# One expert-layer unit reordered: casts queued behind a PSUM copy, a subtraction moved up, weight casts started a step later

## The chip, the cores and the metric

The kernel runs on one core of a Trainium2 chip. The metric is the device time of one execution in microseconds (us); lower is better. Each time is a median of several runs.

## The reference, cut to what matters

The program adds three things: the input `x` of 2048 tokens by 512 features, a spectral filter of the normalised input, and a mixture of 8 experts on the normalised input. Only the experts matter for this change. All 8 experts are used for every token (the "top 8 of 8"), so the work is dense:

```
h = _gelu(jnp.einsum("nd,edf->nef", xt, w1))      # 512 -> 1792 per expert
y = jnp.einsum("nef,efd->ned", h, w2)             # 1792 -> 512
out = jnp.einsum("ne,ned->nd", cw, y)             # weighted by the gates cw
```

Everything is float32, and the result is compared at a precision that the kernel reaches by splitting each matmul operand in two parts.

## The kernel before, in words

**Split operands.** A float32 operand becomes a high part (a cast to the rounded type fp32r, on ScalarE) and a low part (operand minus high part, on VectorE or GpSimd). A product of two such operands is three passes of matmuls: low times high, high times low, high times high. In the code `high()` (L820 is its cast) and `low()` (L823 its subtraction) do this for an activation; `split()` (L549, L550) does it for a weight, with the subtraction on GpSimd.

**Chunks and units.** The 8 x 1792 hidden columns are cut in 56 chunks of 256. Eight chunks are done in the plain way in the first fifth of the run, beside the spectral branch. The other 48 chunks are taken two at a time, as 24 pairs `c`, and for each pair the tokens are taken in two parts `i`; so there are 48 **units** `u = 2c + i`. I call units with `i = 0` even and those with `i = 1` odd. Within a unit the first layer is a 2 x 2 block product done with seven products in place of eight (a Strassen-like scheme): the forms of the input (`b11`, `b21`, `b22`, `T1` to `T4`) lie ready in HBM and are loaded, the forms of the weights (`a11`, `a12`, `a22`, `s1` to `s4`) are made by GpSimd. The second layer is such a block product again, and runs one unit later.

**One product** (`product`, matmuls at L784) is twelve matmuls of 128 x 128 by 128 x 512 into one PSUM tile of 128 x 1024. A unit issues 14 products in this order, numbered P0 to P13 here: first-layer and second-layer products alternate, the second-layer ones being those of the unit before.

- P0 `a11*b11` into X (PSUM tile B); P1 second layer, `b22`; ScalarE copies X to Z (PSUM tile A, L803 `A<-B`).
- P2 `a12*b21` onto X, which the copy must have read by then; P3 second layer, `T3`, onto the tile of P1.
- P4 `s2*T2` onto Z, then a copy of Z to `s` (L803 `c<-A`); P5 second layer, `b11`.
- P6 `s1*T1` onto Z, which the copy to `s` must have read, then a copy to `h22`; P7 second layer, `b21`.
- P8 `s4*b22` onto Z; P9 second layer, `T1`; P10 `s3*T3` into a new tile; P11 second layer, `T4`; P12 `a22*T4`; P13 second layer, `T2`.

**The vector work of a unit.** `gelu` is L807, on ScalarE. `weigh` multiplies by the gates (L838, VectorE). `plus` (L813) adds PSUM to SBUF on VectorE; after every second-layer product it empties or reads the PSUM tile into `acc`, and the next product onto that tile must wait for it. `less` (L816) subtracts two SBUF tiles on VectorE. From the four activated blocks h11, s (the block 21), h22 and h12 these make the second layer's forms: h12 becomes form T3 (`less(h12, h22, h12)`), h11 becomes T1, h22 becomes T2, s becomes T4.

**What sets the order.** In the 48 units the instructions of TensorE, ScalarE and VectorE run in the order in which the code is written (`strict`, `pin`). `layer1` and `layer2` are generators, advanced by the loop at the end of the program: seven rounds of three steps of `layer1`, with one step of the second layer in between, and with some steps of weight preparation (`weights(n)`). In an even unit these prepare the second layer's weights of the pair (sums at L758 to L762, from the tile `raw` loaded as `in_wb`) and stand after the third step of a round; in an odd unit they prepare the first layer's weights of the next pair (L738 to L744, `in_wa`) and stand after the first step. GpSimd's subtractions are placed by the framework's scheduler, in the order of what they wait for. Loads go through one queue, SP's, in order.

Of the kernel before, what the change touches and what calls it, by code (L numbers as in the profile page):

```python
# [89 lines left out]
def r32(ap):  # L90
    return ap.bitcast(F32)
# [3 lines left out]
def body(ctx: ExitStack, tc: tile.TileContext, io):  # L95
    nc = tc.nc
# [6 lines left out]
    scratch = edge.tile([P, EDGE], F32, name="edge")  # L103
# [19 lines left out]
    def load(src):  # L123
        raw = keep.tile([P, 8 * FC], F32, name="raw")
        nc.sync.dma_start(raw, src)
        return raw
# [53 lines left out]
    last_pe, last_dve, last_act, last_pool, main_act, last_cast, last_sp = ([None] for _ in range(7))  # L180
# [149 lines left out]
    def gate(e, i):  # L330

        cb = rp.tile([P, 2, TB], F32, name="cwb", bufs=2)
        for j in range(2):
            c0 = (2 * j + i) * TB
            nc.sync.dma_start(cb[:, j, :], cwd[e, c0 : c0 + TB].partition_broadcast(P))
        return cb
# [208 lines left out]
    def pin(ins):  # L545
        return tc.keep_in_program_order(ins) if strict else ins
# [206 lines left out]
    def sums2(raw, tp, c):  # L753

        a11, a12, a21, a22 = (raw[:, i * F2 : (i + 1) * F2] for i in range(4))
        s1, s2, s4 = (tp.tile([P, F2], F32, name=n) for n in ("s1", "s2", "s4"))
        add = nc.gpsimd.tensor_tensor
        add(s1, a21, a22, op=ALU.add)  # L758
        add(s2, s1, a11, op=ALU.subtract)  # L759
        add(s4, a12, s2, op=ALU.subtract)  # L760
        yield [("s4", s4)] + [("a21", a21)] * (c + 1 == N2)
        add(a21, a21, a11, op=ALU.subtract)  # L762
        yield [("s3", a21)]
        yield [("a11", a11)]
        yield [("a12", a12)]
        yield [("s1", s1)]
        yield [("a22", a22)]
        yield [("s2", s2)]

    def prepare(pool, tag, items, to):  # L770

        for step in items:
            for n, src in step:
                to[n] = pool.tile([P, 2, 2, FC], F32R, name=f"{tag}{n}")
                split(to[n], src.rearrange("p (k f) -> p k f", k=2), nc.gpsimd)
            yield

    def product(pt, w, x, start):

        for m in range(2):  # L780
            n = 0
            for hw, hx in PASSES:
                for k in range(2):
                    pin(nc.tensor.matmul(  # L784
                        pt[:, m, :], w[:, hw, k, m * P : (m + 1) * P], x[:, hx, k, :], start=(start and n == 0), stop=(n == 5),
                        skip_group_check=not start,
                    ))
                    n += 1
# [3 lines left out]
    def bank(name):  # L792
        return pq.tile([P, 2, TB], F32, name=name)

    def xin(n, i):
        if (n, i) in ahead:
            return ahead.pop((n, i))
        x = xr.tile([P, 2, 2, TB], F32R, name="xr", bufs=3)
        nc.sync.dma_start(r32(x), xs[n][i])
        return x  # L800

    def copy_of(dst, src):
        last_act[0] = pin(nc.scalar.copy(dst, src)).ins  # L803
        return dst

    def gelu(v):
        last_act[0] = pin(nc.scalar.activation(v, v, AF.Gelu_apprx_tanh)).ins  # L807

    def tmp():
        return rp.tile([P, 2, TB], F32, name="c", bufs=5)  # L810

    def plus(dst, a, b):
        pin(nc.vector.tensor_add(dst, a, b))  # L813

    def less(dst, a, b):
        pin(nc.vector.tensor_sub(dst, a, b))  # L816

    def high(hs, n, src):
        hs[n] = rp.tile([P, 2, 2, TB], F32R, name="hs", bufs=4)
        main_act[0] = pin(nc.scalar.copy(hs[n][:, 0], src)).ins  # L820

    def low(hs, n, src, pool=False):
        op = (nc.gpsimd if pool else nc.vector).tensor_tensor(hs[n][:, 1], src, r32(hs[n][:, 0]), op=ALU.subtract)  # L823
        if not pool:
            pin(op)
        return op.ins

    def layer1(c, i, w, hs, old):

        last = (c, i) == (N2 - 1, 1)  # L830
        first = c == 0 and i == 0
        e = [ORDER[N1 + 2 * c + j] // NC for j in range(2)]
        cb = {}
        oh, o11, o21, o22, o12 = tuple(old) or (None,) * 5

        def weigh(dst, src, fh, nh):
            g = cb[e[fh]][:, nh : nh + 1, :].to_broadcast([P, 2, TB])
            pin(nc.vector.tensor_mul(dst, src, g))  # L838

        for j in sorted(set(e))[: 1 if first else 2]:  # L840
            cb[j] = gate(j, i)
        X = bank("B")
        x = xin("b11", i)
        product(X, w["a11"], x, True)
        Z = bank("A")
        if first:
            product(Z, w["a11"], x, True)
            ahead["T3", i] = xin("T3", i)
            nc.sync.dma_start(raw, io["wb"][0])
            if e[1] not in cb:  # L850
                cb[e[1]] = gate(e[1], i)
        else:
            copy_of(Z, X)
        yield
        if old:
            low(oh, "T3", o12)
        yield
        if old:
            less(o22, o22, o11)
            high(oh, "T1", o11)  # L860
            low(oh, "T1", o11, True)
        yield

        product(X, w["a12"], xin("b21", i), False)
        gelu(X)
        yield
        if old:
            less(o21, o22, o21)
        h11 = tmp()
        weigh(h11, X, 0, 0)  # L870
        yield
        if old:
            high(oh, "T4", o21)
            low(oh, "T4", o21)
        yield

        product(Z, w["s2"], xin("T2", i), False)
        s = copy_of(tmp(), Z)
        yield
        yield  # L880
        if old:
            high(oh, "T2", o22)
            low(oh, "T2", o22)
        yield

        if first:
            B = bank("B")
            product(B, w["s3"], xin("T3", i), True)
        product(Z, w["s1"], xin("T1", i), False)
        h22 = copy_of(tmp(), Z)  # L890
        yield
        yield
        high(hs, "b11", h11)
        low(hs, "b11", h11, True)
        yield

        product(Z, w["s4"], xin("b22", i), False)
        gelu(Z)
        yield
        h12 = tmp()  # L900
        weigh(h12, Z, 0, 1)
        yield
        if not last:
            less(h11, h12, h11)
        yield

        if not first:
            B = bank("B")
            product(B, w["s3"], xin("T3", i), True)
        plus(h22, B, h22)  # L910
        gelu(h22)
        yield
        weigh(h22, h22, 1, 1)
        yield
        high(hs, "b22", h22)
        yield

        product(B, w["a22"], xin("T4", i), False)
        plus(s, B, s)
        gelu(s)  # L920
        yield
        low(hs, "b22", h22)
        yield
        if not last:
            less(h12, h22, h12)
            high(hs, "T3", h12)
        weigh(s, s, 1, 0)
        high(hs, "b21", s)
        mark = low(hs, "b21", s, True)
        if first:  # L930
            last_pool[0] = mark
        if last:
            high(hs, "b12", h12)
            low(hs, "b12", h12)
        old[:] = hs, h11, s, h22, h12
        yield

# [149 lines left out]
    for u in range(2 * N2):  # L1087
        c, i = divmod(u, 2)
        if u and i == 0:
            raw = load(io["wb"][c])  # L1090
            step2 = prepare(rp, "v", sums2(raw, rp, c), w2q)
        if u == 1:
            ahead.update({(n, 1): xin(n, 1) for n in ("b11", "b21", "T2")})
        if i == 1 and c + 1 < N2:
            raw = load(io["wa"][c + 1])
            step1 = prepare(wq, "u", sums1(raw, wq, False), w1q)
        hs = {}
        one = layer1(c, i, dict(w1q), hs, old)

        def weights(n):  # L1100
            for _ in range(((0, 0, 0, 2, 2, 2, 1) if u < 2 else (0, 1, 1, 1, 1, 1, 2))[n]):
                with tc.issue_after(last_act[0]) if u == 0 else tc.issue_after(last_pool[0]):
                    next(step1 if i else step2, None)

        for n in range(7):
            next(one)
            if i:
                weights(n)
            next(one)
            next(second, None)  # L1110
            next(one)
            if not i:
                weights(n)
        second = layer2(c, i, w2q, hs) if u + 1 < 2 * N2 else layer2_rows(i, w2q, hs)
    strict = False
    last = finish(0)
# [44 lines left out]
```

## Time and profile before

| | us |
|---|---|
| median of 3 runs | 2521.79 (2520.93 to 2527.35) |
| profiled execution, its own time | 2532.53 |
| its span | 2530.7 |
| busy: TensorE matmul | 2369.0 (94%) |
| busy: VectorE | 1691.8 (67%) |
| busy: GpSimd | 1330.4 (53%) |
| busy: ScalarE | 1080.4 (43%) |

The span is what the page's rows add up to. The lines that the prediction shows come from the page, from the list of waits, from the timeline of some 90 us in the middle of the units, and from windows. In a timeline row the first number is the start from the span's begin, the second the time that the instruction (or, with x12, the row of instructions) took; the bracket is the engine's idle time before it and what ended that. A `c` tile is one of five SBUF tiles of a unit, `hs` one of four pairs of high and low parts, `acc` the sum of the experts, `u..` and `v..` the weights of first and second layer.

### The profile page before, as it was taken

How to read it: one execution, taken by the hardware profiler on the slowest of the kernel's cores; microseconds unless marked ns; L12 is line 12 of the kernel's file. 1: busy time of each engine (PE TensorE's matmuls, PEld its weight loads, DVE VectorE, ACT ScalarE, POOL GpSimd, SP SyncE). 2: the span in 40 equal slices, each digit the busy share in tenths (PEclk: the TensorE clock that was granted, in tenths of full speed). 3: DMA queues.
4: the chain of work that ended last, by engine and by line, in shares of the span. 5: the costliest groups of instructions: out<-in, count | busy, mean ns of one | idle time of the engine just before them, and what ended most of it. 6: DMA issues, size and time to landing. Idle time of an engine off the chain costs nothing.

```text
span 2530.7 us, 28405 instructions
## 1 busy us (share of the span) xinstructions
PE 2369.0 (94%) x10736; PEld 1944.4 (77%) x10736; DVE 1691.8 (67%) x1718; ACT 1080.4 (43%) x1529; POOL 1330.4 (53%) x778
## 2 busy tenths in 40 slices
PE   9899999989999999999999999999999999999988
PEld 7687887867777777777787777777777777777877
DVE  7579678636676767676666667666756675767675
ACT  6453443345444444443444444444444444444441
POOL 2123113255656566565756575646564756566561
PEclk9999999999999999999999999999999999999999
DMA  5783522886665566665556566665665665666552
GB/s 194 257 279 108 188 73 74 278 302 244 217 229 209 215 222 232 220 223 203 221 208 222 204 226 213 225 216 216 223 214 199 224 229 207 218 232 233 207 183 100
DMA packets 119416, 530.51 MB, mean 210 GB/s; under 512 B 12112, under 2 KB 30800, under 8 KB 68464
## 3 DMA queue, kind: packets, MB, share of 16 engines
q1 hardware_dynamic: 118480, 515.99, 57.3%
q10 hardware_dynamic: 800, 12.71, 1.5%
q8 instruction: 86, 1.41, 0.2%
q14 instruction: 50, 0.41, 0.0%
HBM read 501.32 MB, written 39.92 MB: 214 GB/s over the span
## 4 chain that ended last, share of the span: by engine, by line
PE 65%; POOL 13%; DMA 8%; DVE 6%; ACT 5%; issue 3%; ACTq 0%; SPq 0%; POOLq 0%; DVEq 0%
PE B L784 21%; PE A L784 16%; PE C L784 13%; PE p L571 5%; PE p L596 5%; DMA raw<-in_wb 4%; POOL hs L823 3%; POOL ua L550 2%; POOL s L759 2%; ACT hs L820 2%; POOL s L758 2%; POOL us L550 1%; DVE c L813 1%; DVE c L816 1%; POOL s L760 1%
## 5 line engine op out<-in xcount | busy, mean ns | idle before, releaser
L823 POOL TENSOR_TENSOR hs<-c,hs 128x1024 fp32r<-128x1024 f32 x143 | 368.2, 2575 | 313.0 <-ACT hs L820 313.0
L784 PE MATMUL B<-xr,ua 128*128 128x512 f32 x1728 | 426.2, 396 | 72.7 <-issue 34.5
L820 ACT CAST hs<-c 128x1024 fp32r<-128x1024 f32 x333 | 350.1, 1052 | 318.0 <-DVE c L816 114.4
L784 PE MATMUL A<-xr,us 128*128 128x512 f32 x1728 | 430.2, 399 | 53.2 <-issue 49.4
L784 PEld LDWEIGHTS B<-xr,ua 128*128 128x128 f32 x1728 | 323.8, 190 | 159.6 <-issue 43.5
L784 PEld LDWEIGHTS A<-xr,us 128*128 128x128 f32 x1728 | 330.3, 192 | 132.4 <-issue 59.6
L784 PE MATMUL C<-hs,vs 128*128 128x512 f32 x1692 | 406.6, 389 | 0.0
L784 PEld LDWEIGHTS C<-hs,vs 128*128 128x128 f32 x1692 | 317.9, 188 | 66.1
L823 DVE TENSOR_TENSOR hs<-c,hs 128x1024 fp32r<-128x1024 f32 x190 | 256.1, 1348 | 99.5 <-ACT hs L820 98.1
L816 DVE TENSOR_TENSOR c<-c 128x1024 f32<-128x1024 f32 x188 | 315.5, 1678 | 9.4 <-POOL hs L823 4.6
L784 PE MATMUL B<-hs,va 128*128 128x512 f32 x1128 | 272.9, 391 | 0.0
L813 DVE TENSOR_TENSOR acc<-B,acc 128x1024 f32<-128x1024 f32 x92 | 112.4, 1222 | 234.1 <-PE B L784 234.1
L813 DVE TENSOR_TENSOR acc<-C,acc 128x1024 f32<-128x1024 f32 x182 | 222.0, 1220 | 46.6 <-PE C L784 46.6
L784 PEld LDWEIGHTS B<-hs,va 128*128 128x128 f32 x1128 | 213.9, 190 | 45.1
L807 ACT ACTIVATE c<-c 128x1024 f32<-128x1024 f32 x96 | 101.8, 1061 | 328.7 <-DVE c L813 328.7
L550 POOL TENSOR_TENSOR h<-c,h 128x512 fp32r<-128x512 f32 (+2 forms) x48 | 54.6, 1152 | 331.5 <-ACT h L549 229.6
L550 POOL TENSOR_TENSOR vs<-s,vs 128x512 fp32r<-128x512 f32 x72 | 115.1, 1599 | 188.9 <-ACT vs L549 188.9
L596 PE MATMUL p<-w,h 128*128 128x512 f32 x768 | 189.7, 398 | 7.5 <-DVE acc L600 4.1
L571 PE MATMUL p<-x,w 128*128 128x512 f32 x768 | 186.1, 395 | 3.5 <-ACT c L580 2.0
L838 DVE TENSOR_TENSOR c<-c,cwb 128x1024 f32<-128x1024 f32 x96 | 143.6, 1496 | 54.0 <-ACT c L807 54.0
L550 POOL TENSOR_TENSOR us<-raw,us 128x512 fp32r<-128x512 f32 x48 | 74.6, 1554 | 199.6 <-ACT us L549 199.6
L596 PEld LDWEIGHTS p<-w,h 128*128 128x128 f32 x768 | 144.6, 191 | 40.2 <-DVE acc L600 6.6
(179 smaller groups left out, 3356.9 us busy)
## 6 DMA issues: line engine op xcount, KB each, us to landing
xr<-xs_T SPq DMA_DIRECT2D x192, 1024.0 KB, 4.8
xr<-xs_b SPq DMA_DIRECT2D x144, 1024.0 KB, 4.8
cwb<-cwd SPq DMA_DIRECT2D x112, 256.0 KB, 6.9
raw<-in_wa SPq DMA_DIRECT2D x24, 1024.0 KB, 5.0
raw<-in_wb SPq DMA_DIRECT2D x24, 1024.0 KB, 4.9
tab<-cbd SPq DMA_DIRECT2D x32, 384.0 KB, 4.0
raw<-in_wp SPq DMA_DIRECT2D x16, 512.0 KB, 5.0
xs_T<-Y SPq DMA_DIRECT2D x8, 1024.0 KB, 7.4
```

The source lines that it names most:

```text
L550: return (eng or nc.vector).tensor_tensor(dst[:, 1], src, r32(dst[:, 0]), op=ALU.subtract).ins
L571: last = nc.tensor.matmul(p1, w1[k][:, hw, f * P : (f + 1) * P], x, start=(n == 0), stop=(n == 11))
L596: last = nc.tensor.matmul(p2, h[f][:, hh, js], w2[f][:, hw], start=(n == 0), stop=(n == 6 * NFT - 1))
L758: add(s1, a21, a22, op=ALU.add)
L759: add(s2, s1, a11, op=ALU.subtract)
L784: pin(nc.tensor.matmul(pt[:, m, :], w[:, hw, k, m * P : (m + 1) * P], x[:, hx, k, :], start=(start and n == 0), stop=(n == 5), skip_group_ ...
L807: last_act[0] = pin(nc.scalar.activation(v, v, AF.Gelu_apprx_tanh)).ins
L813: pin(nc.vector.tensor_add(dst, a, b))
L816: pin(nc.vector.tensor_sub(dst, a, b))
L820: main_act[0] = pin(nc.scalar.copy(hs[n][:, 0], src)).ins
L823: op = (nc.gpsimd if pool else nc.vector).tensor_tensor(hs[n][:, 1], src, r32(hs[n][:, 0]), op=ALU.subtract)
L838: pin(nc.vector.tensor_mul(dst, src, g))
```

## The change

Three edits in the unit, and one in the table of weight steps.

1. The cast of form `b21` and its low part move from the end of a unit to the next unit's second step, behind the copy of X to Z. The low part of `T3` takes the place at the unit's end, so `T3` is complete there.
2. `less(h12, h22, h12)`, which makes form T3, moves one step up, ahead of the low part of `b22`. In the next unit `weigh(h11)` is now written ahead of `less(o21, o22, o21)`, since the latter overwrites the tile that the low part of `b21` reads.
3. The weight steps by round change from (0,1,1,1,1,1,2) to (0,1,1,1,1,2,1) in odd units and (0,0,1,1,1,2,2) in even units.
4. Things that go with it: a one-column GpSimd copy in the first unit serves as the marker that the low part of `b21` was; in the last unit the low part of `b21` is on VectorE.

```
-            low(oh, "T3", o12)
+            high(oh, "b21", o21)
+            low(oh, "b21", o21, True)
...
+        h11 = tmp()
+        weigh(h11, X, 0, 0)
         if old:
             less(o21, o22, o21)
-        h11 = tmp()
-        weigh(h11, X, 0, 0)
...
-        low(hs, "b22", h22)
-        yield
         if not last:
             less(h12, h22, h12)
-            high(hs, "T3", h12)
-        weigh(s, s, 1, 0)
-        high(hs, "b21", s)
-        mark = low(hs, "b21", s, True)
-        if first:
-            last_pool[0] = mark
+        low(hs, "b22", h22)
+        yield
         if last:
+            weigh(s, s, 1, 0)
+            high(hs, "b21", s)
+            low(hs, "b21", s)
             high(hs, "b12", h12)
             low(hs, "b12", h12)
+        else:
+            high(hs, "T3", h12)
+            low(hs, "T3", h12)
+            weigh(s, s, 1, 0)
+        if first:
+            last_pool[0] = nc.gpsimd.tensor_copy(scratch[:, :1], h12[:, 0, :1]).ins
...
-            for _ in range(((0, 0, 0, 2, 2, 2, 1) if u < 2 else (0, 1, 1, 1, 1, 1, 2))[n]):
+            for _ in range(((0, 0, 0, 2, 2, 2, 1) if u < 2 else (0, 1, 1, 1, 1, 2, 1) if i else (0, 0, 1, 1, 1, 2, 2))[n]):
```

How the rows move on three engines:

ScalarE where an even unit begins, before. `A<-B` is the copy of X to Z; of the casts, c_10245 is h12 (form T3), c_10168 is s (form b21, further down form T4), c_10136 is h11 (form T1); `vs4` is the second layer's first weight cast.

```order
L807 ACTIVATE c_10168<-c_10168 128x1024
L549 CAST us3_10314<-raw_10072 128x512
L549 CAST ua22_10317<-raw_10072 128x512
L820 CAST hs_10336<-c_10245 128x1024
L820 CAST hs_10339<-c_10168 128x1024
L803 COPY A_10362<-B_10347 128x1024
L820 CAST hs_10380<-c_10136 128x1024
L807 ACTIVATE B_10347<-B_10347 128x1024
L820 CAST hs_10414<-c_10168 128x1024
L549 CAST vs4_10423<-s4_10419 128x512
L803 COPY c_10440<-A_10362 128x1024
```

The same place now (s is c_10169 here, h12 c_10246):

```order
L807 ACTIVATE c_10169<-c_10169 128x1024
L549 CAST ua22_10318<-raw_10071 128x512
L820 CAST hs_10337<-c_10246 128x1024
L803 COPY A_10361<-B_10346 128x1024
L820 CAST hs_10363<-c_10169 128x1024
L820 CAST hs_10381<-c_10136 128x1024
L807 ACTIVATE B_10346<-B_10346 128x1024
L820 CAST hs_10415<-c_10169 128x1024
L803 COPY c_10432<-A_10361 128x1024
L820 CAST hs_10448<-c_10205 128x1024
L549 CAST vs4_10457<-s4_10453 128x512
```

The cast of b21 now stands behind the copy to Z, one of the weight casts has gone from in front of it, and the cast of `vs4` now stands behind the copy of Z to s.

VectorE at the same place, before (c_10204 is h22; C, A and B are PSUM tiles):

```order
L813 TENSOR_TENSOR c_10168<-B_10262,c_10168 128x1024
L823 TENSOR_TENSOR hs_10296<-c_10204,hs_10296 128x1024
L813 TENSOR_TENSOR acc_5021<-A_10321,acc_5021 128x1024
L816 TENSOR_TENSOR c_10245<-c_10204,c_10245 128x1024
L838 TENSOR_TENSOR c_10168<-c_10168,cwb_10074 128x1024
L823 TENSOR_TENSOR hs_10336<-c_10245,hs_10336 128x1024
L813 TENSOR_TENSOR acc_5021<-C_10365,acc_5021 128x1024
L816 TENSOR_TENSOR c_10204<-c_10204,c_10136 128x1024
L816 TENSOR_TENSOR c_10168<-c_10204,c_10168 128x1024
L838 TENSOR_TENSOR c_10399<-B_10347,cwb_10344 128x1024
```

And now:

```order
L813 TENSOR_TENSOR c_10169<-B_10263,c_10169 128x1024
L816 TENSOR_TENSOR c_10246<-c_10205,c_10246 128x1024
L823 TENSOR_TENSOR hs_10300<-c_10205,hs_10300 128x1024
L813 TENSOR_TENSOR acc_5021<-A_10323,acc_5021 128x1024
L823 TENSOR_TENSOR hs_10337<-c_10246,hs_10337 128x1024
L838 TENSOR_TENSOR c_10169<-c_10169,cwb_10073 128x1024
L813 TENSOR_TENSOR acc_5021<-C_10366,acc_5021 128x1024
L816 TENSOR_TENSOR c_10205<-c_10205,c_10136 128x1024
L838 TENSOR_TENSOR c_10399<-B_10346,cwb_10343 128x1024
L816 TENSOR_TENSOR c_10169<-c_10205,c_10169 128x1024
```

The subtraction for T3 goes two places up, the weighing of s goes behind the low part of T3, and the last two rows change places.

GpSimd where an odd unit begins, before (c_9899 is s, c_9858 is h11):

```order
L550 TENSOR_TENSOR vs1_10025<-s1_9876,vs1_10025 128x512
L823 TENSOR_TENSOR hs_10063<-c_9899,hs_10063 128x1024
L550 TENSOR_TENSOR va22_10066<-raw_9801,va22_10066 128x512
L550 TENSOR_TENSOR vs2_10069<-s2_9877,vs2_10069 128x512
L823 TENSOR_TENSOR hs_10110<-c_9858,hs_10110 128x1024
L738 TENSOR_TENSOR s1_10128<-raw_10072 128x512
```

And now (s is c_9891):

```order
L550 TENSOR_TENSOR vs1_10026<-s1_9910,vs1_10026 128x512
L550 TENSOR_TENSOR va22_10065<-raw_9800,va22_10065 128x512
L550 TENSOR_TENSOR vs2_10068<-s2_9911,vs2_10068 128x512
L823 TENSOR_TENSOR hs_10093<-c_9891,hs_10093 128x1024
L823 TENSOR_TENSOR hs_10111<-c_9858,hs_10111 128x1024
L738 TENSOR_TENSOR s1_10129<-raw_10071 128x512
```

The low part of b21 now comes behind two weight subtractions, and directly ahead of the low part of T1.

More of the change, by code (lines that the diff above doesn't have):

```diff
@@ L921, in layer1 @@
         yield
+        if not last:
+            less(h12, h22, h12)
         low(hs, "b22", h22)
         yield
-        if not last:
-            less(h12, h22, h12)
-            high(hs, "T3", h12)
-        weigh(s, s, 1, 0)
-        high(hs, "b21", s)
-        mark = low(hs, "b21", s, True)
-        if first:
-            last_pool[0] = mark
         if last:
+            weigh(s, s, 1, 0)
+            high(hs, "b21", s)
+            low(hs, "b21", s)
             high(hs, "b12", h12)
             low(hs, "b12", h12)
+        else:
[4 more added lines that the diff above has]
+            last_pool[0] = nc.gpsimd.tensor_copy(scratch[:, :1], h12[:, 0, :1]).ins
         old[:] = hs, h11, s, h22, h12
```

## The prediction

> **What bounds the kernel now.** I read the page first: TensorE is busy 94% of the span, and the chain that ended last is TensorE for 65% of it.
>
> ```profile
> PE 2369.0 (94%) x10736; PEld 1944.4 (77%) x10736; DVE 1691.8 (67%) x1718; ACT 1080.4 (43%) x1529; POOL 1330.4 (53%) x778
> PE 65%; POOL 13%; DMA 8%; DVE 6%; ACT 5%; issue 3%; ACTq 0%; SPq 0%; POOLq 0%; DVEq 0%
> ```
>
> So only TensorE's gaps can be won. Next, the list of waits for that engine; three groups stand out, one per pair of units each.
>
> ```profile
> PE A L784 <- issue: 49.4, 22, 2.3
> PE B L784 <- issue: 34.5, 23, 1.6
> PE B L784 <- ACT A L803: 31.0, 24, 3.4
> ```
>
> Then the timeline, to see which products these are: TensorE's over one pair, an even unit from 1324.62 and an odd one from 1368.70.
>
> ```profile
> 1324.62 2.88 PE L784 MATMUL B<-xr,ua 128*128 128x512 f32 x12
> 1327.34 2.88 PE L784 MATMUL C<-hs,vs 128*128 128x512 f32 x12
> 1331.78 2.98 PE L784 MATMUL B<-xr,ua 128*128 128x512 f32 x12 [1.55 <-issue]
> 1334.60 2.88 PE L784 MATMUL C<-hs,vs 128*128 128x512 f32 x12
> ...
> 1345.22 4.45 PE L784 MATMUL A<-xr,us 128*128 128x512 f32 x12 [2.30 <-issue]
> ...
> 1368.70 2.88 PE L784 MATMUL B<-xr,ua 128*128 128x512 f32 x12
> 1371.42 2.88 PE L784 MATMUL C<-hs,vs 128*128 128x512 f32 x12
> 1375.53 3.03 PE L784 MATMUL B<-xr,ua 128*128 128x512 f32 x12 [1.23 <-ACT A L803]
> ```
>
> Undisturbed products start 2.72 apart (1324.62 to 1327.34). The stalls are P2 of both units and P6 of the even one. ScalarE's timeline in the even unit shows why:
>
> ```profile
> 1329.72 1.05 ACT L820 CAST hs<-c 128x1024 fp32r<-128x1024 f32 x1 [1.18 <-DVE c L838]
> 1330.67 1.01 ACT L803 COPY A<-B 128x1024 f32<-128x1024 f32 x1
> ...
> 1337.52 1.06 ACT L820 CAST hs<-c 128x1024 fp32r<-128x1024 f32 x1 [1.71 <-PE C L784]
> 1343.59 0.62 ACT L549 CAST vs<-s 128x512 fp32r<-128x512 f32 x1 [5.02 <-POOL s L760]
> 1344.12 1.00 ACT L803 COPY c<-A 128x1024 f32<-128x1024 f32 x1
> ```
>
> A consumer can start 2.92 after a product's start (1334.60 to the cast at 1337.52). So P0 is ready for its copy near 1327.54, but the copy starts at 1330.67, behind the cast of b21, which waited for a weighing; P2 follows at 1331.78. The copy of Z to s could start near 1340.24 (P4 is due 2.72 after 1334.60), but stands behind a weight cast that waits for GpSimd's third sum; P6 follows. In the odd unit the copy has the two form casts and two weight casts in front of it:
>
> ```profile
> 1371.36 2.17 ACT L820 CAST hs<-c 128x1024 fp32r<-128x1024 f32 x2 [2.87 <-DVE c L816]
> 1373.44 0.61 ACT L549 CAST va<-raw 128x512 fp32r<-128x512 f32 x1
> 1373.95 0.61 ACT L549 CAST vs<-s 128x512 fp32r<-128x512 f32 x1
> 1374.47 1.00 ACT L803 COPY A<-B 128x1024 f32<-128x1024 f32 x1
> ```
>
> **What all stalls together are worth.** The steady part runs from unit 2's P0 to the end of unit 47's P13:
>
> ```profile
> 584.59 2.88 PE L784 MATMUL B<-xr,ua 128*128 128x512 f32 x12
> 2486.21 2.89 PE L784 MATMUL A<-hs,vs 128*128 128x512 f32 x12
> ```
>
> That is 2486.21 + 2.72 - 584.59 = 1904.3. Its 46 units of 14 products at 2.72 (38.08 each) need 1751.7. So 152.7 can be won, 6.64 per pair. The three wait groups are 114.9 of it; the other 38 is the restart after each stall, and products that run slowly after one: the one at 1345.22 took 4.45, and TensorE's granted clock (the 0.64) was down there:
>
> ```profile
> 1345.20:1349.50 4.30, 4.28 (x13) 3.40 (x14) 1.23 (x1) 1.39 (x2) 2.16 (x2) 0.64 0.00 0
> ```
>
> So I let those 38 go with the stalls.
>
> **A resource that the change leans on.** SP's, GpSimd's and VectorE's timelines in the two units:
>
> ```profile
> 1328.57 0.33 SPq L125 DMA_DIRECT2D raw<-in_wb  x1
> ...
> 1330.84 2.38 POOL L823 TENSOR_TENSOR hs<-c,hs 128x1024 fp32r<-128x1024 f32 x1 [2.30 <-ACT hs L820]
> 1331.82 4.71 DVE L816 TENSOR_TENSOR c<-c 128x1024 f32<-128x1024 f32 x2
> 1333.41 2.04 POOL L758 TENSOR_TENSOR s<-raw 128x512 f32<-128x512 f32 x1 [0.19 <-DMA raw<-in_wb]
> ...
> 1342.28 1.28 POOL L760 TENSOR_TENSOR s<-raw,s 128x512 f32<-128x512 f32 x1
> ...
> 1370.04 1.22 DVE L816 TENSOR_TENSOR c<-c 128x1024 f32<-128x1024 f32 x1
> 1371.17 1.22 DVE L838 TENSOR_TENSOR c<-c,cwb 128x1024 f32<-128x1024 f32 x1
> 1378.18 2.27 POOL L550 TENSOR_TENSOR vs<-s,vs 128x512 fp32r<-128x512 f32 x1
> 1379.64 1.23 DVE L838 TENSOR_TENSOR c<-B,cwb 128x1024 f32<-128x1024 f32 x1 [0.34 <-ACT B L807]
> ```
>
> Two subtractions on VectorE at 1331.82 took 4.71, where one alone takes 1.22 (1370.04). GpSimd's op of 1330.84 ends at 1333.22; the first subtraction fits behind it, GpSimd's op of 1333.41 then takes 2.04 where its like took 1.28 (1342.28), then comes the second: the two engines take turns, whole instructions long. A VectorE op that reads PSUM (1379.64) ran beside GpSimd's without loss. I take alone: 1.22 on VectorE (1.13 to the next, from 1370.04 to 1371.17), 1.29 for GpSimd's 512, 2.38 for its 1024, and first come first served.
>
> **The change, part by part**, with times from the unit's P0 and due times at 2.72 each.
>
> *Even unit.* At its start GpSimd has one weight subtraction left. VectorE makes h12's subtraction (ready at -1.3, done -0.2), the low part of b22 (0.9; P1 at 2.72 needs it), then reads P13 (2.1). The copy to Z now also waits for that read, but P0 ends later: copy 2.96 to 3.97, P2 due 5.44. The stall goes, with 1.4 to spare. The low part of T3 ends at 3.3, the weighing of s at 4.4, the cast of b21 at 5.5, its low part on GpSimd 5.6 to 8.0. The subtraction for o22 follows at 9.1, GpSimd's first weight sum 10.35 (`in_wb`, issued near 2.2 in place of 3.95, has landed at 7 by the 4.84 from 1328.57 to 1333.41), GpSimd's low part of T1 12.7, and only then VectorE's `less(o21)` 13.9. ScalarE's cast of T4 waits for it (15.0), and the copy to s is behind that: 14.9 to 15.9, where P6, due 16.32, needs it. No stall, 0.35 to spare. The cast of vs4 waits for the third sum at 18.8; behind it the copy to h22 runs 19.4 to 20.4, due 21.76. Both stalls of the even unit are gone.
>
> *Odd unit.* Here the table leaves GpSimd va12 and vs1 just before (-2.7 to -0.2) and va22 and vs2 just after. h12's subtraction waits until -0.2 and ends at 1.0, the low part of b22 2.1, the read of P13 3.3, the copy to Z 4.3: P2's stall goes, 1.0 to spare. But now T3's low part waits for va22 (ends 5.1), the weighing of s for vs2 (6.3 to 7.5), and the read of P1's tile is queued behind it: 7.4 to 8.6. P3, due 8.16, starts at 8.7: 0.55 late. Cast of b21 8.6, `less(o22)` 9.7, low part of b21 12.0, of T1 14.4, `less(o21)` 15.6, cast of T4 16.6, copy to s 17.6; P6, now due 16.87, starts at 17.66. In all 1.34 late, where the odd unit now loses 1.54 (1375.53 - 1371.42 - 2.72, and 0.15 more in P2). So here a stall is moved, not removed. Its bounds: 0 if the engines did not block each other, 2.6 if GpSimd goes one more op of 1.29 ahead.
>
> *Loads and the rest.* `in_wa` is issued when va22 is done, near 4, and so earlier than now; the load of T1 passes behind it on SP, but is needed only at 16.3 and takes 4.8 to land. No instruction is added but a one-column copy and, in the last unit, one swap of engines: at most a us either way. In the last unit two GpSimd ops now stand ahead of b21's low part:
>
> ```profile
> 2446.00 3.30 POOL L989 TENSOR_TENSOR acc<-acc 128x1024 f32<-128x1024 f32 x1 [2.86 <-DVE acc L813]
> ```
>
> With these, its P6 is about 5 late by the same walk.
>
> **Sum.** 152.7 - 22 odd units x 1.34 (29.5) - 5 = 118. The profiled execution, 2532.53, would be 2414; the median lies 10.7 below it, and 2521.79 - 118 = **2404**.
>
> **Rivals.**
>
> *No new wait* (0.20): the waits of the odd unit vanish, since the low part of T1 misses its turn or the weight casts come a little earlier. Then `less(o21)` can end near 11.8 and the copy to s is on time. 152.7 less the last unit's: 2374 at most, 2369 with that gone too. For it: ScalarE and VectorE have the time. Against it: the turns seen at 1331.82. [...]
>
> *Both units pay* (0.18): one more GpSimd op of 1.29 goes ahead of `less(o21)` in each: the even unit loses 0.95, the odd one 2.6, 3.55 per pair. 152.7 - 22 x 3.55 - 5 = 70: 2452. For it: the even unit has 0.35 only.
>
> *The copy to Z stays late* (0.06), so that the change does not do what it says: it now waits for VectorE's read of P13, which has a subtraction more in front of it. Three turns lost to GpSimd (3 x 1.29) would keep P2 as it is; only P6's stall of 2.46 in even units goes, 23 x 2.46 = 57: 2465.
>
> *The slow products stay* (0.02): if the clock of 0.64 had another cause than the idling ahead of it, the 38 would not come: 118 - 38 = 80, or 2442. Against it: the row begins straight after 2.30 of idling, and nothing else changed there. [...]
>
> *Slower* (0.04): the cast of T4 in front of the copy to s becomes the clock of every unit. GpSimd's b21, T1 and two sums all go first; the odd unit loses 4.0, the even one 2.3, and 1.5 more as the third sum makes the copy to h22 late. 7.8 per pair against 6.64 is slower by 27: 2549. It decides from a loss of 6.64 per pair on. Against it: all ops of both engines there, placed end to end from 2.7, end at 14.4.
>
> **How the numbers follow.** The forecast itself has 0.50, for 2390 to 2420. The range 2368 to 2455 takes in the first two rivals and the slow products, and leaves out about 0.13. Differences within 0.3% (8 us) can hardly be told from none. Faster 0.94, within 0.02, slower 0.04.
>
> **What would show it.** In the list of waits the groups of P2 and of the even P6 are gone; the odd units show a short wait at P6 for ScalarE's copy, with the cast of T4 directly ahead of it and `less(o21)` ending with GpSimd's low part of T1, and perhaps one at P3 for VectorE. No product runs at a clock of 0.64 but in the last units. The mean period of a pair falls from 82.8 (76.16 + 6.64) to about 77.5. I am wrong if P2 still waits, if even units stall as much as odd ones, or if the odd ones run through.

## The result, and the profile after

The changed kernel takes 2410.44 us (median of 4 runs, 2407.06 to 2411.45) where the kernel before took 2521.36 beside it (4 runs, 2520.51 to 2527.35). The ratio is 0.9553, with an interval of 0.9535 to 0.957: 110.9 us less. The forecast was 2404, with 2390 to 2420 for the forecast itself. The profiled execution of the change took 2410.91, and its span is 2409.1.

On the page of the kernel after, TensorE's busy time fell by 20.9 and its share rose to 97%. VectorE's rose by 93 with one instruction more: its instructions take longer, 1.04 on the mean (1784.9 over 1719) in place of 0.98 (1691.8 over 1718).

```profile
PE 2348.1 (97%) x10736; PEld 1935.9 (80%) x10736; DVE 1784.9 (74%) x1719; ACT 1080.7 (45%) x1529; POOL 1334.4 (55%) x778
```

TensorE's waits, in the list of waits of the kernel after (total, times, longest), start like this:

```profile
PE A L784 <- ACT c L803: 13.0, 24, 3.8
PE C L784 <- DVE acc L813: 7.2, 23, 0.6
PE B L784 <- DVE c L813: 6.4, 2, 5.1
```

The three groups of before (49.4, 34.5 and 31.0) are gone. Two small ones have come, each about once per pair; the third group is two waits in the first units. TensorE's timeline shows where the two are, in an odd unit from 1318.80 and the even unit behind it from 1358.12:

```profile
1318.80 2.88 PE L784 MATMUL B<-xr,ua 128*128 128x512 f32 x12
1321.52 2.88 PE L784 MATMUL C<-hs,vs 128*128 128x512 f32 x12
1324.24 2.88 PE L784 MATMUL B<-xr,ua 128*128 128x512 f32 x12
1327.42 3.00 PE L784 MATMUL C<-hs,vs 128*128 128x512 f32 x12 [0.30 <-DVE acc L813]
...
1336.23 3.02 PE L784 MATMUL A<-xr,us 128*128 128x512 f32 x12 [0.36 <-ACT c L803]
...
1358.12 2.88 PE L784 MATMUL B<-xr,ua 128*128 128x512 f32 x12
...
1363.56 2.88 PE L784 MATMUL B<-xr,ua 128*128 128x512 f32 x12
...
1374.44 2.88 PE L784 MATMUL A<-xr,us 128*128 128x512 f32 x12
...
1404.82 3.00 PE L784 MATMUL C<-hs,vs 128*128 128x512 f32 x12 [0.30 <-DVE acc L813]
```

P2 waits in neither unit (5.44 after P0 in both), and the even unit's P6 starts 16.32 after its P0, when it is due. The odd unit's P3 and P6 wait. From one odd unit's P3 (1327.42) to the next one's (1404.82) is 77.40. Without waits a pair takes 76.16, so 1.24 are lost per pair, all in the odd unit. The granted clock is 1.00 in the windows over the steady part, of which this is one (window, length, then busy us of TensorE, weight loads, VectorE, ScalarE and GpSimd, the clock, DMA share and GB/s):

```profile
1500.00:2000.00 500.00, 496.01 (x2175) 406.93 (x2174) 386.35 (x273) 231.29 (x271) 329.73 (x180) 1.00 0.65 234
```

### The profile page after: what moved, and what is told of

Read it like the earlier page. It is cut to its first block, busy times and chain, and to the rows that moved or that the text cites. A ratio compares the mean times of both kernels' runs of the same rounds, so it can differ in the third digit from the quotient of the medians.

```text
span 2409.1 us, 28455 instructions
## 1 busy us (share of the span) xinstructions
PE 2348.1 (97%) x10736; PEld 1935.9 (80%) x10736; DVE 1784.9 (74%) x1719; ACT 1080.7 (45%) x1529; POOL 1334.4 (55%) x778
## 5 line engine op out<-in xcount | busy, mean ns | idle before, releaser
L823 POOL TENSOR_TENSOR hs<-c,hs 128x1024 fp32r<-128x1024 f32 x142 | 359.9, 2540 | 210.9 <-ACT hs L820 199.2
L784 PE MATMUL A<-xr,us 128*128 128x512 f32 x1728 | 419.7, 392 | 14.0 <-ACT c L803 13.0
L784 PE MATMUL B<-xr,ua 128*128 128x512 f32 x1728 | 418.0, 391 | 7.2 <-DVE c L813 6.4
L784 PEld LDWEIGHTS A<-xr,us 128*128 128x128 f32 x1728 | 323.2, 188 | 90.9 <-ACT c L803 21.6
L816 DVE TENSOR_TENSOR c<-c 128x1024 f32<-128x1024 f32 x188 | 375.7, 1998 | 10.2 <-POOL hs L823 10.1
L823 DVE TENSOR_TENSOR hs<-c,hs 128x1024 fp32r<-128x1024 f32 x191 | 299.7, 1570 | 5.6 <-ACT hs L820 2.5
L550 POOL TENSOR_TENSOR va<-raw,va 128x512 fp32r<-128x512 f32 x73 | 95.2, 1304 | 235.8 <-ACT va L549 235.8
L571 PEld LDWEIGHTS p<-x,w 128*128 128x128 f32 x768 | 144.5, 190 | 32.9 <-ACT c L580 2.0
```

What stands on the lines that cost most here:

```text
L550: return (eng or nc.vector).tensor_tensor(dst[:, 1], src, r32(dst[:, 0]), op=ALU.subtract).ins
L571: last = nc.tensor.matmul(p1, w1[k][:, hw, f * P : (f + 1) * P], x, start=(n == 0), stop=(n == 11))
L784: pin(nc.tensor.matmul(pt[:, m, :], w[:, hw, k, m * P : (m + 1) * P], x[:, hx, k, :], start=(start and n == 0), stop=(n == 5), skip_group_ ...
```

## Experiments

Each kernel was timed against the kernel before in the same rounds, so ratios are given. The kernel before has a median of 2523.37 beside the first three below and the one with the casts of `b21` early, and of 2525.87 beside the others.

### The table alone

The kernel before, with only the new table of weight steps:

```
-  ... else (0, 1, 1, 1, 1, 1, 2))[n]):
+  ... else (0, 1, 1, 1, 1, 2, 1) if i else (0, 0, 1, 1, 1, 2, 2))[n]):
```

> The kernel before with the new table of weight steps alone. Theory A (each stall has its own cause; the even unit's P6 waits because the cast of vs4 stands in front of the copy to s): the even P6 stall goes, both P2 stalls stay at about 1.5 and 1.2 in the list of waits; gain 22 x 2.46 and most of the slow products, about 75 us: 2447 (2435 to 2465). Rival B (the copy freed from the cast of b21 is the whole gain, the table only tidies): 2505 to 2520.

Measured: 2462.64, ratio 0.9754 (0.973 to 0.9778), about half of the gain. The even P6 no longer waits. P2 is the only place left in the steady units, shown by the list of waits of this kernel:

```profile
PE B L784 <- ACT A L803: 46.5, 24, 4.1
PE B L784 <- issue: 10.6, 23, 0.7
```

Its TensorE timeline has the even unit's P2 and the odd one's:

```profile
1303.83 2.99 PE L784 MATMUL B<-xr,ua 128*128 128x512 f32 x12 [0.45 <-issue]
...
1344.10 4.25 PE L784 MATMUL B<-xr,ua 128*128 128x512 f32 x12 [1.92 <-ACT A L803]
```

The time lies inside the expected range, 16 above its middle, but its parts came out otherwise: the even P2 fell from 1.55 to 0.45, and the odd one rose from 1.23 to 1.92. The new table is later in even units only; in odd units one of the seven steps stands a round earlier. So GpSimd has two weight subtractions just ahead of an odd unit (here that of 1336.57) where it had one (in that of 1368.70 before), and VectorE's low part of `b22`, which starts beside them, takes 2.37 in place of 1.22. All that follows on the two engines slides, and the copy to Z starts 6.47 after P0 in place of 5.77, which is the rise. The rows agree with this; that it is the cause was not tried by itself. Of the 22 products behind such a stall of 1.92, 7 ran slowly, like the one at 1344.10.

### Everything but the table

The change with the old table:

```
-  ... else (0, 1, 1, 1, 1, 2, 1) if i else (0, 0, 1, 1, 1, 2, 2))[n]):
+  ... else (0, 1, 1, 1, 1, 1, 2))[n]):
```

> The change with the old table of weight steps. Theory A: P2 no longer waits, but in the even unit the copy to s is still behind the cast of vs4, which waits for GpSimd's third sum near 18.8 to 19.5 after P0 whatever TensorE does; P6 then starts near 20.5 after P0 as it does before the change (20.6), a stall of about 4 in place of 1.8 and 2.5. Longer stalls slow more products, odd units gain a little: about 2515 (2495 to 2535), so nearly nothing of the gain. Rival B: 2410 to 2425.

Measured: 2539.47, ratio 1.0046 (1.0026 to 1.0067). All of the edit but the table makes the kernel slower, by about half a per cent. P2 is free, but all that is won there is lost at the even P6. The list of waits of this kernel has its total:

```profile
PE A L784 <- issue: 89.8, 20, 4.6
```

ScalarE's timeline of this kernel, ahead of one such P6:

```profile
1350.46 0.62 ACT L549 CAST vs<-s 128x512 fp32r<-128x512 f32 x1 [5.80 <-POOL s L760]
1350.98 1.01 ACT L803 COPY c<-A 128x1024 f32<-128x1024 f32 x1
```

And TensorE's, with that P6, which waits 4.55 where it waited 2.30 before the change:

```profile
1352.09 5.46 PE L784 MATMUL A<-xr,us 128*128 128x512 f32 x12 [4.55 <-issue]
```

The copy to `s` still stands behind the cast of `vs4`, and that waits for GpSimd's third sum. In this unit that sum ends 19.4 after P0, where it ended 18.9 after P0 in the unit of 1324.62 before the change. So with P2 free TensorE only waits longer at P6. The stall was expected at about 4 and measures 4.55; the time lies above the range of 2495 to 2535. What was undersized in the main is the products after a stall: 24 rows in the steady part took over 3.5 (the 5.46 is one), 47.9 us above their 2.88 in all, where the kernel before has 10 with 15.8. The mean clock of this execution is 0.972, against 0.987.

### The subtraction for T3 late again

The change with `less(h12, h22, h12)` back behind the low part of `b22`:

```
-        if not last:
-            less(h12, h22, h12)
         low(hs, "b22", h22)
         yield
+        if not last:
+            less(h12, h22, h12)
```

> The change with less(h12, h22, h12) back at its old place, behind the low part of b22 and the read of P13. Theory A: form T3's cast comes 1.1 to 2.3 later and stands in front of the copy to Z, in odd units with two weight casts; P2 is about 1 late there again, and the later weighing of s makes the copy to s later, in even units too (about 1): 3.1 per pair in place of 1.24: 2453 (2425 to 2465). Rival B: no difference, 2405 to 2415.

Measured: 2484.64, ratio 0.9843 (0.9813 to 0.9873), outside the expected range. The odd unit's P2 waits 0.81, where about 1 was foreseen. The even unit's P2 does not wait, though about 1 was expected there too, but its P6 waits 1.85 on the mean, in this kernel's list of waits:

```profile
PE A L784 <- issue: 43.7, 24, 3.0
PE B L784 <- ACT A L803: 18.6, 23, 0.8
```

One such P6, of an even unit, and the next odd unit's P2, in its TensorE timeline:

```profile
1323.84 4.58 PE L784 MATMUL A<-xr,us 128*128 128x512 f32 x12 [1.95 <-issue]
...
1353.71 3.01 PE L784 MATMUL B<-xr,ua 128*128 128x512 f32 x12 [0.81 <-ACT A L803]
```

GpSimd's timeline in this kernel, from the start of the even unit whose P6 that is, shows an order that the edit does not name:

```profile
1312.20 1.30 POOL L758 TENSOR_TENSOR s<-raw 128x512 f32<-128x512 f32 x1 [5.11 <-DMA raw<-in_wb]
1313.58 2.16 POOL L759 TENSOR_TENSOR s<-s,raw 128x512 f32<-128x512 f32 x1
1315.69 1.30 POOL L762 TENSOR_TENSOR raw<-raw 128x512 f32<-128x512 f32 x1
1316.94 2.40 POOL L823 TENSOR_TENSOR hs<-c,hs 128x1024 fp32r<-128x1024 f32 x1
```

Three weight sums stand ahead of the low part of `b21` (the L823). GpSimd's order is not written out but chosen by the scheduler, and the subtraction's new place made it choose otherwise. So this run mixes two things, and one more was made to part them.

### The same, with GpSimd's order held

As above, and the weight steps told to come after the low part of `b21`:

```
-            low(oh, "b21", o21, True)
+            last_pool[0] = low(oh, "b21", o21, True)
```

> The run with less(h12, h22, h12) at its old place, 2484.64, had GpSimd's low part of b21 behind three weight sums in the even units, since the framework's scheduler put it there; here the weight steps are told to come after that low part, so that GpSimd's order is that of the change. Theory E (that order made the even unit's P6 1.95 late and slowed its product): the even P6 is at most 1 late, the odd unit as before it (P2 0.81, P6 0.38); about 2445 (2430 to 2460). Rival (the late subtraction itself costs it): 2478 to 2490.

Measured: 2446.59, ratio 0.9687 (0.9657 to 0.9717). That is 38 below the run without the order held, and 36 above the change by the medians (34 by the ratios). Rows of this kernel's TensorE timeline (an even unit's P6 and P8, then the next odd unit's P2 and P6):

```profile
1312.82 2.88 PE L784 MATMUL A<-xr,us 128*128 128x512 f32 x12
...
1319.28 3.03 PE L784 MATMUL A<-xr,us 128*128 128x512 f32 x12 [0.86 <-ACT c L803]
...
1342.16 3.02 PE L784 MATMUL B<-xr,ua 128*128 128x512 f32 x12 [0.81 <-ACT A L803]
...
1353.70 3.01 PE L784 MATMUL A<-xr,us 128*128 128x512 f32 x12 [0.35 <-ACT c L803]
```

The even P6 now starts when it is due. The odd unit's waits are as in the run above. What waits in the even unit is P8, for the copy to `h22`: that copy stands behind the cast of `vs4`, and the third sum, which the cast needs, ends 21.2 after P0 here (P0 at 1296.49), against 18.3 in the change (P0 at 1358.12). So the moved subtraction itself is worth some 35 us. The rest of the loss above came from GpSimd's order.

### The casts of b21 early again

The change with `b21` cast at the end of the unit, and the low part of `T3` back in the next unit:

```
         if old:
-            high(oh, "b21", o21)
-            low(oh, "b21", o21, True)
+            low(oh, "T3", o12)
...
             high(hs, "T3", h12)
-            low(hs, "T3", h12)
             weigh(s, s, 1, 0)
+            high(hs, "b21", s)
+            low(hs, "b21", s, True)
```

> The change with the cast of b21 and its low part back at the end of the unit, in front of the copy, and T3's low part in the next unit; subtraction and table as changed. Theory A: the moved subtraction alone brings the weighing of s forward by some 1 us, so the even unit's P2 hardly waits; the odd one's waits about 2 (weighing, cast of b21, two weight casts, copy end near 7.5 where 5.44 is due), while P3 and P6 no longer wait: about 2.2 per pair in place of 1.24, 2432 (2415 to 2450). Rival B: most of the gain is lost, 2480 to 2515.

Measured: 2430.02, ratio 0.9621 (0.9599 to 0.9643). Only the odd unit's P2 waits, as in the kernel before, for the copy behind the cast. The list of waits of this kernel:

```profile
PE B L784 <- ACT A L803: 44.3, 23, 1.9
```

And that P2 in its TensorE timeline:

```profile
1333.26 3.03 PE L784 MATMUL B<-xr,ua 128*128 128x512 f32 x12 [1.93 <-ACT A L803]
```

The time is as expected, and P3 and P6 run through here. So the cast behind the copy is worth 17 us by the ratios, or 20 by the medians, of the 111, and the stalls that it moves to P3 and P6 are taken off that already.

### The cast of T4 behind the copy to s

The prediction put the odd P6 down to the cast of T4 directly ahead of the copy to `s`. Here that cast and its low part stand behind the copy:

```
         yield
-        if old:
-            high(oh, "T4", o21)
-            low(oh, "T4", o21)
         yield
...
         yield
+        if old:
+            high(oh, "T4", o21)
+            low(oh, "T4", o21)
         yield
```

> The change with the cast of T4 and its low part written behind the copy to s. Theory A (the odd unit's P6 waits because the cast of T4, itself waiting for less(o21) and GpSimd's lows, stands in front of the copy to s on ScalarE): the waits of P6 go, in the last unit too (3.8 there), those of P3 for VectorE stay at 0.30; period of a pair 76.7 in place of 77.4; 2392 (2386 to 2400). Rival C (the copy to s is late for a reason of its own, or the wait moves to P7, whose tile VectorE reads behind T4's low part): 2405 to 2415.

Measured: 2406.98, ratio 0.9533 (0.9508 to 0.9558), which is no gain on the change that these runs can tell from none. The wait at P6 is gone, as theory A has it, but the time is rival C's, and for the second of its two reasons: P7 waits in P6's place. The list of waits of this kernel:

```profile
PE B L784 <- POOL raw L743: 9.1, 22, 0.5
PE C L784 <- DVE acc L813: 6.9, 23, 0.3
```

Its VectorE timeline:

```profile
1334.15 1.96 DVE L823 TENSOR_TENSOR hs<-c,hs 128x1024 fp32r<-128x1024 f32 x1 [0.51 <-ACT hs L820]
1336.04 1.21 DVE L813 TENSOR_TENSOR acc<-B,acc 128x1024 f32<-128x1024 f32 x1
```

And TensorE's, with P7:

```profile
1337.40 3.00 PE L784 MATMUL B<-hs,va 128*128 128x512 f32 x12 [0.41 <-POOL raw L743]
```

The list names GpSimd, whose instruction happened to end then. P7 goes onto P5's tile, and so needs VectorE's read of it; that read ends at 1337.25. It is queued behind the low part of T4, which took 1.96. A wait put down to an engine that does not touch the tile is to be read with the queue of the one that does.

### The even unit's weight steps one round earlier

The chain of the odd unit's lateness begins at its start, where GpSimd has two weight subtractions in turn with VectorE. One more change of the table, in even units only, lets two of the seven weight steps come a round earlier:

```
-  ... if i else (0, 0, 1, 1, 1, 2, 2))[n]):
+  ... if i else (0, 0, 1, 1, 2, 2, 1))[n]):
```

> The change with the even units' weight steps one earlier, (0,0,1,1,2,2,1): one weight subtraction in place of two stands on GpSimd where the odd unit begins. Theory A (VectorE and GpSimd take turns, and the odd unit's waits are the turns): the weighing of s ends near 6.2 in place of 7.3 after P0, P3 no longer waits for VectorE, P6 waits 0.1 to 0.4; period 76.3 to 76.8; 2393 (2385 to 2400). Rival D (P3 waits because VectorE has one op more in its own queue, whatever GpSimd does): P3 still waits 0.30; 2405 to 2413.

Measured: 2381.55 (2379.28 to 2383.56), ratio 0.943 (0.9405 to 0.9456): 28.9 below the change by the medians, 31 by the ratios, and the fastest kernel of this study. That is below the expected range of 2385 to 2400: P6 was expected to keep a wait of 0.1 to 0.4, and does not. In a window of 500 us of the steady units TensorE is busy for all of it (columns as above):

```profile
1500.00:2000.00 500.00, 500.00 (x2205) 413.29 (x2204) 385.76 (x277) 236.28 (x277) 337.05 (x183) 1.00 0.66 237
```

The groups of P3 and P6 are gone from its list of waits (each waits in the first pair and in the last unit only), and the first row is now that of the first units:

```profile
PE B L784 <- DVE c L813: 6.4, 2, 5.1
```

The cause shows in two timelines at the start of an odd unit. First GpSimd's of the change (P0 at 1318.80):

```profile
1321.54 1.29 POOL L550 TENSOR_TENSOR va<-raw,va 128x512 fp32r<-128x512 f32 x1 [2.84 <-ACT va L549]
1322.79 2.27 POOL L550 TENSOR_TENSOR vs<-s,vs 128x512 fp32r<-128x512 f32 x1
```

VectorE's of the change, in the same stretch:

```profile
1321.98 1.93 DVE L823 TENSOR_TENSOR hs<-c,hs 128x1024 fp32r<-128x1024 f32 x1
1323.84 2.30 DVE L838 TENSOR_TENSOR c<-c,cwb 128x1024 f32<-128x1024 f32 x1
1326.06 1.21 DVE L813 TENSOR_TENSOR acc<-C,acc 128x1024 f32<-128x1024 f32 x1
```

Then GpSimd's of this kernel (P0 at 1386.04):

```profile
1387.62 1.65 POOL L550 TENSOR_TENSOR vs<-s,vs 128x512 fp32r<-128x512 f32 x1 [0.58 <-ACT vs L549]
```

And VectorE's of this kernel:

```profile
1389.18 1.21 DVE L823 TENSOR_TENSOR hs<-c,hs 128x1024 fp32r<-128x1024 f32 x1
1390.31 1.21 DVE L838 TENSOR_TENSOR c<-c,cwb 128x1024 f32<-128x1024 f32 x1
1391.68 1.23 DVE L813 TENSOR_TENSOR acc<-C,acc 128x1024 f32<-128x1024 f32 x1 [0.16 <-PE C L784]
```

VectorE's order is the same in both. With one GpSimd subtraction left after P0 in place of two, the low part of T3 takes 1.21, not 1.93, the weighing 1.21, not 2.30. The read of P1's tile, queued behind them, then waits only for P1 itself. The expectation gave P3's wait two readings; the one by which it stays whatever GpSimd does is refuted.

### Both together

The cast of T4 behind the copy, and the last table:

> Both of the two runs before together. Theory A: no wait of over 0.1 is left in the steady units, the period of a pair is 76.2, that is 14 products at 2.72 twice; 2379 (2374 to 2388). Rivals C and D: no better than the better one of the two alone, 2392 to 2410.

Measured: 2385.34, ratio 0.9447 (0.9419 to 0.9475), inside the expected range but not better than the last table without the moved cast. P6 had nothing left to win, and the waits are not all below 0.1: in 8 units P7 now waits, by this kernel's list of waits:

```profile
PE B L784 <- POOL ua L550: 5.9, 8, 0.8
```

## Why the prediction was right, and what it missed

**What bounds the kernel, and what is to win.** Right. TensorE's stalls in the steady part were all that could be won. From unit 2's P0 to the end of unit 47's P13 the change takes:

```profile
584.15 2.88 PE L784 MATMUL B<-xr,ua 128*128 128x512 f32 x12
2366.93 2.89 PE L784 MATMUL A<-hs,vs 128*128 128x512 f32 x12
```

2366.93 + 2.72 - 584.15 = 1785.5, which is 118.8 less than the 1904.3 of before. The sum of the prediction was 118. The kernel of the last table, almost without waits, confirms the other end. Its span is 27.3 below the change's (2409.1 to 2381.8). Its first 22 pairs take 76.30 on the mean where the change's take 77.41, which is 24.4 of this, and its last unit takes 40.7 in place of 44.4.

**Even unit.** Right: both stalls are gone. ScalarE's row of the copy to `s` (P0 at 1358.12):

```profile
1372.87 1.00 ACT L803 COPY c<-A 128x1024 f32<-128x1024 f32 x1
```

It runs 14.75 to 15.75 after P0, where 14.9 to 15.9 was forecast and 16.32 is the due time.

**Odd unit.** Right, in the mechanism and nearly in size: 1.24 lost per pair for 1.34. The walk and the rows, in us after P0 (the measured side is the unit of 1318.80):

| | forecast | measured |
|---|---|---|
| copy of X to Z | 3.3 to 4.3 | 3.3 to 4.3 |
| low part of T3 ends | 5.1 | 5.1 |
| weighing of s ends | 7.5 | 7.3 |
| read of P1's tile ends | 8.6 | 8.5 |
| P3 starts (due 8.16) | 8.7 | 8.62 |
| `less(o21)` ends | 15.6 | 15.3 |
| cast of T4 ends | 16.6 | 16.5 |
| copy to `s` ends | 17.6 | 17.4 |
| P6 starts | 17.66 | 17.43 |

Two rows of ScalarE show the queue at P6, the cast of T4 after its wait for `less(o21)` and the copy behind it:

```profile
1334.21 1.05 ACT L820 CAST hs<-c 128x1024 fp32r<-128x1024 f32 x1 [4.53 <-DVE c L816]
1335.17 1.00 ACT L803 COPY c<-A 128x1024 f32<-128x1024 f32 x1
```

The run with the cast behind the copy adds something to this: the cast was the last in that line, not the only one. Taking it away moved the wait to P7.

**Two engines in turn.** Right, and here shown by a run: the last table takes one GpSimd subtraction out of the turn and leaves VectorE's order as it was. The low part of T3 then takes 1.21 in place of 1.93 and the weighing 1.21 in place of 2.30, and both waits (0.30 at P3 and 0.36 at P6 in the change) go. The rival without new waits needed what that table does and the change does not. Neither the rival in which both units pay nor the late copy to Z came true.

**Last unit.** Its P6 was put at about 5 late. It starts 4.5 later than due (20.84 after the unit's P0 at 2325.29, for 16.32), and its own wait is 3.8. With the slow product behind it the unit loses 6.3:

```profile
2346.13 4.35 PE L784 MATMUL A<-xr,us 128*128 128x512 f32 x12 [3.80 <-ACT c L803]
```

**Slow products.** Right that they go with the stalls: over the windows of the steady part the clock is 1.00, where it was 0.98 to 1.00 before, and the one row left of over 3.5, of 4.35, is that of the last unit.

**What was mis-sized** is the last line of the sum, "the median lies 10.7 below it". The profiled execution of before was 10.7 above its median, and I took the gain worked out from that execution off the median as it was. The profiled execution of the change is only 0.5 above its own. Between the two profiles lie 121.6 us (2532.53 to 2410.91), between the medians 110.9. The runs of the kernel before bear on what the 10.7 are. Their times go with their granted clock: 2518.8 at 0.992, 2523.37 at 0.990, 2530.73 at 0.987, 2532.49 at 0.985. This fits with executions that differ by how many products ran slowly after a stall. The profiled one would then have had more of them than most, and since the change takes the stalls away, the excess was counted as won from the median too, which had less of it. This is argued from the clocks: no trace of another execution of this kernel was kept. In the profiled one the 10 slow products of the steady part cost 15.8, so the 10.7 would be some seven of them. Had the 10.7 been taken off the 38 for restarts and slow products, the forecast would have been 2414 for the median as well, and the miss 4 in place of 6, in the other direction. Between the profiles the sum of 118 was 3.6 short of 121.6, so the mechanism holds a little better than the time of the median shows.

**Which part earned what.** The prediction costed the edits together, and the runs show why that was needed. The table alone wins 2.5%, the rest without it loses 0.5%, and the whole wins 4.5%. The table takes the wait for GpSimd's third sum out of ScalarE's queue ahead of the copy to `s`; only then is the time won at P2 kept.

## What to carry to other kernels

Price an edit by the next wait on the same chain: everything but the table freed P2 and still made this kernel slower, until the table took the next stall away. Where two engines take turns, as VectorE and GpSimd do here (the weighing of s took 2.30 with a GpSimd subtraction of 2.27 beside it and 1.21 without one), walk both queues in order of time, instruction by instruction; that walk came within 0.3 us at every step of the odd unit here, and taking one GpSimd subtraction from the right place, by a change of the table, was then worth 29 us. And when a gain is worked out from one profiled execution, ask whether the distance of that execution from the median is made of the very thing that the change removes.

## What was not expected of the hardware

How long a stall has to be before the products behind it run slowly. Counting the stalls from unit 2 on by length, and the product rows of over 3.5 us behind them (2.88 to 3.06 is usual), over the kernels above:

| stall, us | kernel | slow behind it |
|---|---|---|
| 1.2 to 1.6 | before | 0 of 44 |
| 1.7 to 1.80 | late subtraction | 0 of 12 |
| 1.83 to 1.84 | late subtraction | 3 of 3 |
| 1.9 | late subtraction | 4 of 5 |
| 1.9 | table alone | 7 of 22 |
| 1.9 | b21 early | 1 of 23 |
| 2.0 to 2.1 | late subtraction | 2 of 2 |
| 2.3 | before | 9 of 21 |
| 2.6 | cast of T4 behind | 0 of 1 |
| 3.0 to 4.1 | five kernels | 7 of 7 |
| 4.5 to 4.6 | old table | 21 of 21 |

In this count no stall of 1.80 or less slowed the product behind it, and every one of 3.0 or more did. Between 1.83 and 2.6 it differs at the same length. What goes with it there is the moment at which the product starts. Divide the start of each such product by 3.4133 us and keep the remainder:

| kernel | slow | usual |
|---|---|---|
| before, stalls of 2.3 | 9 at 0.06 to 1.88 | 12 at 2.16 to 3.35 |
| table alone, 1.9 | 7 at 2.67 to 3.15 | 15 at 1.02 to 2.55 |
| b21 early, 1.9 | 1 at 1.00 | 22 at 2.00 to 2.96 |
| late subtraction, 1.83 to 2.1 | 9 at 1.56 to 2.89 | 1 at 0.07 |

The remainders of two kernels cannot be compared, since each trace has a start of its own. The period is an estimate from the first two rows: of all periods from 1.5 to 14 us in steps of 0.0001, only 3.4130 to 3.4138 part the slow ones from the usual ones, into one stretch each, in both. The other two rows were not used to find it. How slow the product is goes by the remainder too: in the table-alone kernel the seven take 4.25 at 2.67 and more and more up to 4.61 at 3.15, and in the old table, where all are slow, those behind 4.5 to 4.6 take 5.46 at 0.12 to 0.42, 4.58 or 4.59 at 2.05 to 2.23, and 4.41 to 4.49 at 2.83 to 3.02. So in these traces the slowing follows a beat of about 3.41 us that does not start anew with a stall, and a stall of 1.83 to 2.3 us, shorter than the beat, counts or not by where it falls on it. No run was made to try this.

For a forecast it means that a kernel with stalls of about 2 us can have a time that scatters by more than others do: 14 us between the runs of before in one session (2518.8 to 2532.49), against 2.5 to 9.3 for the five kernels whose steady pairs have no stall of over 1.8. The other four lie between (4.9 to 8.6), so only the kernel before shows it. And removing such stalls can win more than their length, as their slow products go too: in the steady part the 10 of before cost 15.8 us, the one left in the change 1.5.
